# Moving part of w2's last block to an earlier load on 32 partitions, and w_mod in two loads

## The chip, the core and the metric

The kernel runs on one core of one Trainium2 chip. The metric is the time of one execution on the device in microseconds (us). Beside it each execution reports its *span*, the time from the first to the last recorded instruction of the core. Time minus span is called *overhead* below. The engines are named as in the profile: PE multiplies matrices, DVE and ACT work on vectors, POOL does small side work, SP issues the loads. A load is split over up to sixteen DMA engines; each moves its share in *packets* and, when it is through, posts a *landing* (in the trace of before, the load w2[16:24] has sixteen, from 411.48 to 413.60 us). The last landing of a load releases whoever waits for it (there PE starts at 413.65 us). All executions that were timed in rounds are counted as fast ones, and on one core there is no slower die to sort out.

## The reference, cut to what matters

```python
mod = (silu(c) @ w_mod).reshape(2, 6, 1, -1)            # w_mod: 1024 x 6144
h = layernorm(x) * (1 + ca) + sa                        # x: 2 x 1 x 1024
x = x + ga * attention(h, k_cache, v_cache, wq, wo)     # 32 heads on 4 KV heads, 32768 keys
h = layernorm(x) * (1 + cb) + sb
x = x + gb * (gelu(layernorm(h) @ w1 + b1) @ w2 + b2)   # w1: 1024 x 3584, w2: 3584 x 1024
```

Two rows of x go through one transformer block. Everything else is weights and cache: 178.3 MB have to be read, and each byte is used once.

## The kernel before

All large loads are issued by SyncE into one queue, in one fixed order, each as soon as its place in memory is free. w_mod comes first, in three loads of 1, 3 and 4 blocks of k. w2 comes last, in five.

```python
WMOD_ITEMS = ((0, 1), (1, 4), (4, 8))
W2_ITEMS = ((0, 8, 96), (8, 16, 112), (16, 24, 0), (24, 27, 16), (27, 28, 22))  # from block, to block, place
...
for k0, k1 in WMOD_ITEMS:
    add(("wmod", k0), [k1 - k0, 6 * DM], wm_v[:, k0:k1, :], k0 * 12 * KB)
# wq, then K and V of 8 groups, then wo, then w1
w2_v = B_w2.rearrange("(p j) n -> p j n", j=FT)          # FT = 28 blocks, DM = 1024
for m, (j0, j1, off) in enumerate(W2_ITEMS):
    add(("w2", m), [j1 - j0, DM], w2_v[:, j0:j1, :], off * KB)
```

The end of the kernel. Blocks 16 to 27 of w2 are used as weights of small matmuls with two columns; what follows is short and serial.

```python
for g in range(16, FT):
    m, j = w2_of[g]
    it = need("w2", m)                                    # waits for this load
    for k in range(KT8):                                  # KT8 = 8
        pe(lambda e, ...: e.matmul(psO[:, 2 * k:2 * k + 2], lhsT=w[:, j, k * 128:(k + 1) * 128], rhs=gT[:, g, 0:2],
                                   start=False, stop=(g == FT - 1), ...), ...)
dve(... mT = psO * mod(5));  dve(... res_bf = mT + x1b)
pe(... psM = res_bf transposed);  dve(... res16 = psM)
...
T.wait("sp", reads=["res16"])
T.raw("sp", lambda e: e.dma_start(out..., res16[:, :]).then_inc(s_out, 16))
...
nc.sync.wait_ge(s_out, 16)                                # the program ends when the output is in memory
```

Of the kernel before, what the change touches and what calls it, by code (L numbers as in the profile page):

```python
# [8 lines left out]
BF16 = mybir.dt.bfloat16  # L9
# [5 lines left out]
DM = 1024  # L15
KT8 = DM // 128
F = 3584
FT = F // 128
# [15 lines left out]
RING = 160 * 1024  # L34
KC_AT = 128 * 1024
AHEAD = ("sc2", "sc3", "pk", "ac")
WMOD_ITEMS = ((0, 1), (1, 4), (4, 8))
W2_ITEMS = ((0, 8, 96), (8, 16, 112), (16, 24, 0), (24, 27, 16), (27, 28, 22))
KEEP = {(0, 1): 0, (0, 3): 1, (0, 5): 2, (1, 1): 3}

# [196 lines left out]
def bass_adaLN_cond__gqa_block_cached__mixer_channel_mlp__decode_kernel(  # L237
# [15 lines left out]
    T = Tracker(nc)  # L253
    T.step["pe"], T.step["dve"] = 74, 18

    def sb(name, shape, dtype=FP32):
        return nc.alloc_sbuf_tensor(name, list(shape), dtype)

    ident = sb("ident", [128, 128], BF16)
# [41 lines left out]
    gT = sb("gT", [128, FT, 32], BF16)  # L301
    mT = sb("mT", [128, KT8, 2])
    res_bf = sb("res_bf", [128, 2, KT8], BF16)
    res16 = c16
    m1c = sb("m1c", [128, HPG, NCH])
    m1 = sb("m1", [128, HPG])
    gm = sb("gm", [HPG, 1])
# [25 lines left out]
    psO = psZ[:, 1, :]  # L333
    psM = nc.alloc_psum_tensor("psM", [128, 512], FP32)
# [8 lines left out]
    KB = 1024  # L343

    def add(key, shape, src, off, slot=None, sem=None, view=None):
        it = Item()
        it.key, it.n = key, len(stream)
        it.off, it.nbytes = off, int(np.prod(shape)) * 2
        assert off + it.nbytes <= RING
        it.reg = f"it{it.n}"  # L350
        it.sem = f"d_{sem or slot or it.reg}"
        it.view = views.get(slot) if view is None else view
        if it.view is None:
            it.view = nc.alloc_sbuf_tensor_at(f"{key[0]}_{it.n}", [128] + list(shape), BF16, offset=abase + off)
            if slot:
                views[slot] = it.view
        it.src = src
        stream.append(it)
        by_key[key] = it
# [31 lines left out]
        add(("w1", m), [4, F], w1_v[:, 4 * m:4 * m + 4, :], off * KB)  # L391
    w2_v = B_w2.rearrange("(p j) n -> p j n", j=FT)
    for m, (j0, j1, off) in enumerate(W2_ITEMS):
        add(("w2", m), [j1 - j0, DM], w2_v[:, j0:j1, :], off * KB)
    w2_of = {j: (m, j - j0) for m, (j0, j1, off) in enumerate(W2_ITEMS) for j in range(j0, j1)}

    kc = nc.alloc_sbuf_tensor_at("kc", [128, 2, TPC * D], BF16, offset=abase + KC_AT)
# [18 lines left out]
    def dve(fn, reads=(), writes=(), sem=None):  # L416
        T.inst("dve", fn, reads=reads, writes=writes, sem=sem)
# [4 lines left out]
    def pe(fn, reads=(), writes=(), mark=True):  # L422
        T.inst("pe", fn, reads=reads, writes=writes, mark=mark)
# [5 lines left out]
    for t, nm in ((ident, "ident"), (identf, "identf")):  # L429
        T.inst("pool", lambda e, t=t: e.memset(t[:, :], 0.0), writes=[nm])  # L430
        T.inst("pool", lambda e, t=t: e.affine_select(out=t[:, :], in_=t[:, :], compare_op=ALU.not_equal, fill=1.0,
                                                      base=0, pattern=[[-1, 128]], channel_multiplier=1), reads=[nm], writes=[nm])
    T.inst("pool", lambda e: e.memset(onesf[:, :], 1.0), writes=["onesf"])
    for t, nm in [(inT, "inT"), (gT, "gT")] + [(atT[g], f"atT{g}") for g in range(G // 2)]:
        T.inst("pool", lambda e, t=t: e.memset(t[:, :, :], 0.0), writes=[nm])

    for k in range(KT8):
        pe(lambda e, k=k: e.matmul(psM[:, 2 * k:2 * k + 2], lhsT=c2[:, k::KT8], rhs=ident[0:2, 0:2], start=True, stop=True),
           reads=["KT_sb0", "ident"], writes=["psM"], mark=False)
# [46 lines left out]
    for k in range(KT8):  # L486
        k0, kk = wmod_of[k]
        it = need("wmod", k0)
        for ch in range(12):
            n, q = ch // 4, ch % 4  # L490
            pe(lambda e, w=it.view, k=k, kk=kk, ch=ch, n=n, q=q: e.matmul(bank[n][32 * q:32 * q + 32, :], lhsT=inT[:, k, :], rhs=w[:, kk, ch * 512:(ch + 1) * 512],  # L491
                                                                   start=(k == 0), stop=(k == KT8 - 1), skip_group_check=True),
# [227 lines left out]
    for m in range(2):  # L720
        it = need("wo", m)
        for j in range(16):
            for hf in range(2):
# [2 lines left out]
                                                                       start=(m == 0 and j < 2), stop=(m == 1 and j >= 14), skip_group_check=True),  # L726
                   reads=[it.reg, f"atT{m}"], writes=["psS0"], mark=(j == 15 and hf == 1))

    def load_row(e_name, b, b_reg, n, parts=128):
        dst, src = row[0:parts, n * 512:(n + 1) * 512], b[0:parts, :]  # L730
        if e_name == "act":
            act(lambda e: e.activation(dst, src, ACT.Copy), reads=[b_reg], writes=[f"row{n}"] + ROW)
        else:
            dve(lambda e: e.tensor_copy(dst, src), reads=[b_reg], writes=[f"row{n}"] + ROW)

    def to_columns(dst, d_reg, n, start, mark):
        for i in range(4):
            pe(lambda e, i=i: e.matmul(dst[:, 2 * i:2 * i + 16].rearrange("p (h r) -> p h r", r=8)[:, :, 0:2], lhsT=row[:, n * 512 + i * 128:n * 512 + (i + 1) * 128],
                                       rhs=half[:, :, :], start=(start and i == 0), stop=True, skip_group_check=True),
               reads=[f"row{n}", "half"] + ROW, writes=[d_reg], mark=(mark and i == 3))  # L740
# [51 lines left out]
               reads=[it.reg, "gT"], writes=["psS0"], mark=(hf == 1 and g in (7, 15)))  # L792
    load_row("dve", psS[0], "psS0", 3)
    to_columns(psO, "psO", 3, True, False)
    for g in range(16, FT):
        m, j = w2_of[g]
        it = need("w2", m)
        for k in range(KT8):
            pe(lambda e, w=it.view, g=g, j=j, k=k: e.matmul(psO[:, 2 * k:2 * k + 2], lhsT=w[:, j, k * 128:(k + 1) * 128], rhs=gT[:, g, 0:2],  # L799
                                                            start=False, stop=(g == FT - 1), skip_group_check=True),  # L800
               reads=[it.reg, "gT"], writes=["psO"], mark=(k == KT8 - 1 and g in (23, 26, 27)))
    dve(lambda e: e.tensor_tensor(mT[:, :, :], psO[:, 0:16].rearrange("p (k b) -> p k b", b=2), mod(5), ALU.mult), reads=["psO", "modT"], writes=["mT"])
    dve(lambda e: e.tensor_tensor(res_bf.rearrange("p b k -> p k b"), mT[:, :, :], x1b[:, :, :], ALU.add), reads=["mT", "x1b"], writes=["res_bf"])
    pe(lambda e: e.matmul(psM[0:16, 0:128], lhsT=res_bf.rearrange("p b k -> p (b k)"), rhs=ident[:, :], start=True, stop=True),
# [38 lines left out]
```

## Time and profile before

| what | before |
|---|---|
| time, median of 3 (range) | 420.06 us (419.78 to 420.2) |
| span of the profiled execution | 419.0 us |
| bytes read | 178.28 MB, 425 GB/s over the span |
| latest landing of w2[16:24] | 413.60 us |
| from there to the end of the span | 5.40 us |
| instruction blocks fetched (16 KB each) | 8 |

The pages of the profile are read from the end backwards. The last row of work is a chain: the load w2[16:24] lands, PE works through 96 small matmuls, DVE multiplies and adds, PE transposes, DVE copies, and the 4 KB result is stored. Whatever moves the time must move the landing of w2[16:24], or something behind it. The lines themselves stand in the prediction below.

### The profile page before, as it was taken

What the parts mean: (1) busy time and instruction counts of PE and PEld (TensorE: products, weight loads), DVE (VectorE), ACT (ScalarE), POOL (GpSimd) and SP (SyncE); (2) the same over time, 40 slices, a digit from 0 to 9 for tenths busy, and PEclk for the clock granted to TensorE, in tenths of its full rate; (3) what the DMA queues carried; (4) which work ended last, traced back from release to release, by engine and by line L of the source; (5) the groups of instructions that cost most, each with busy time, mean ns of one, the idle gap of its engine ahead of it and who ended that gap; (6) DMA issues with size and microseconds to landing.
All of it is one profiled execution on the core that took longest, in us unless ns stands there. A gap on an engine that the chain in (4) does not pass through costs nothing.

```text
span 419.0 us, 11898 instructions
## 1 busy us (share of the span) xinstructions
PE 291.7 (70%) x5215; PEld 234.7 (56%) x5215; DVE 246.1 (59%) x535; ACT 181.8 (43%) x219; POOL 6.8 (2%) x29
## 2 busy tenths in 40 slices
PE   1407445878599578939885995798398839966466
PEld 1104114874499378719854993687198539932324
DVE  1201101856786877778577768777885868683421
ACT  2000012555277537715862775378248716750100
POOL 3000000000000000000000000000000000000000
PEclk9966656798799969988987999699889968996565
DMA  9999999999999999999999999999999999999995
GB/s 369 448 391 443 444 408 491 408 409 460 413 432 450 419 432 450 438 413 450 438 413 457 432 413 457 432 413 463 432 407 463 432 407 463 404 416 443 422 429 230
DMA packets 4573, 178.42 MB, mean 426 GB/s; under 512 B 586, under 2 KB 594, under 8 KB 852
## 3 DMA queue, kind: packets, MB, share of 16 engines
q1 hardware_dynamic: 4564, 178.28, 98.6%
q8 instruction: 8, 0.13, 0.1%
q14 instruction: 1, 0.01, 0.0%
HBM read 178.28 MB, written 0.00 MB: 425 GB/s over the span
## 4 chain that ended last, share of the span: by engine, by line
DMA 60%; PE 22%; DVE 9%; issue 5%; ACT 3%; SPq 0%; ACTq 0%; DVEq 0%
DMA kv<-in_A_k_cache_dram 45%; PE psKT L560 13%; DMA wmod<-in_w_mod_dram 7%; DMA w<-in_B_w_dram 7%; ACT KT_sb L564 3%; DVE KT_sb L566 3%; PE psS L577 2%; DVE m1c L581 2%; DVE kc L571 2%; PE psZ L629 1%; PE psZ L577 1%; DVE msum L652 1%; PE psS L725 1%; PE psZ L491 1%; PE psZ L799 1%
## 5 line engine op out<-in xcount | busy, mean ns | idle before, releaser
L564 ACT ACTIVATE KT_sb<-psKT 128x1024 bf16<-128x1024 bf16 x128 | 128.3, 1024 | 96.7 <-PE psKT L560 96.7
L566 DVE COPY KT_sb<-psKT 128x1024 bf16<-128x1024 bf16 x128 | 88.0, 689 | 59.7 <-PE psKT L560 59.4
L560 PE MATMUL psKT<-ident,kv 128*128 128x128 bf16 x1024 | 90.5, 248 | 10.9 <-DMA kv<-in_A_k_cache_dram 10.9
L560 PEld LDWEIGHTS psKT<-ident,kv 128*128 128x128 bf16 x1024 | 73.3, 113 | 12.8 <-DMA kv<-in_A_k_cache_dram 12.8
L560 PE MATMUL psKT<-ident,kc 128*128 128x128 bf16 x1024 | 77.9, 218 | 0.0
L560 PEld LDWEIGHTS psKT<-ident,kc 128*128 128x128 bf16 x1024 | 58.1, 97 | 1.9 <-issue 1.7
L577 PE MATMUL psS<-qcur,KT_sb 128*128 128x8 bf16 x1024 | 45.1, 167 | 10.1 <-DVE KT_sb L566 6.0
L577 PE MATMUL psZ<-qcur,KT_sb 128*128 128x8 bf16 x1024 | 42.1, 167 | 11.2 <-ACT KT_sb L564 10.7
L577 PEld LDWEIGHTS psS<-qcur,KT_sb 128*128 128x128 bf16 x1024 | 40.2, 98 | 11.9 <-DVE KT_sb L566 6.3
L577 PEld LDWEIGHTS psZ<-qcur,KT_sb 128*128 128x128 bf16 x1024 | 36.8, 96 | 13.4 <-ACT KT_sb L564 12.7
L571 DVE COPY kc<-kv 128x4096 bf16<-128x4096 bf16 x32 | 39.0, 1217 | 8.1 <-DMA kv<-in_A_k_cache_dram 8.1
L629 PE MATMUL psZ<-V,E_sb 128*32 128x512 bf16 x384 | 28.3, 414 | 2.0 <-ACT E_sb L603 2.0
L603 ACT ACTIVATE E_sb<-S_sb 128x512 bf16<-128x512 f32 x32 | 19.2, 626 | 16.1 <-DVE S_sb L601 16.1
L601 DVE TENSOR_TENSOR S_sb<-S_sb,gmb 128x512 f32<-128x512 f32 x32 | 21.3, 687 | 0.5
L642 PE MATMUL psM<-onesf,rsum 128*128 128x1 f32 x16 | 3.4, 281 | 25.9 <-DVE rsum L639 25.9
L608 DVE TENSOR_REDUCE rs<-E_sb 128x8 f32<-128x512 bf16 x32 | 20.9, 675 | 0.0
L642 PEld LDWEIGHTS psM<-onesf,rsum 128*128 128x128 f32 x16 | 2.7, 212 | 29.9 <-DVE rsum L639 29.9
L582 ACT ACTIVATE S_sb<-psS 128x512 f32<-128x512 f32 x16 | 9.6, 597 | 20.4 <-DVE m1c L581 20.4
L491 PE MATMUL psS<-wmod,inT 128*32 128x512 bf16 x32 | 4.9, 606 | 17.0 <-DMA wmod<-in_w_mod_dram 17.0
L629 PEld LDWEIGHTS psZ<-V,E_sb 128*32 128x32 bf16 x384 | 11.0, 102 | 9.5 <-ACT E_sb L603 2.7
L657 PE MATMUL psM<-msum,hmat 128*128 128x128 f32 x16 | 6.4, 501 | 13.3 <-DVE msum L652 13.3
L499 DVE COPY S_sb<-psS 128x512 f32<-128x512 f32 x1 | 0.7, 692 | 23.2 <-PE psS L491 23.2
(139 smaller groups left out, 237.4 us busy)
## 6 DMA issues: line engine op xcount, KB each, us to landing
wq<-in_A_wq_dram SPq DMA_DIRECT2D x2, 4096.0 KB, 44.7
kv<-in_A_k_cache_dram SPq DMA_DIRECT2D x2, 4096.0 KB, 37.7
wo<-in_A_wo_dram SPq DMA_DIRECT2D x2, 4096.0 KB, 20.6
w<-in_B_w_dram SPq DMA_DIRECT2D x2, 3584.0 KB, 23.5
wmod<-in_w_mod_dram SPq DMA_DIRECT2D x1, 6144.0 KB, 29.9
w<-in_B_w_dram SPq DMA_DIRECT2D x3, 2048.0 KB, 29.2
wmod<-in_w_mod_dram SPq DMA_DIRECT2D x1, 4608.0 KB, 15.9
wmod<-in_w_mod_dram SPq DMA_DIRECT2D x1, 1536.0 KB, 6.2
```

Of the source, the lines that this page charges most:

```text
L491: pe(lambda e, w=it.view, k=k, kk=kk, ch=ch, n=n, q=q: e.matmul(bank[n][32 * q:32 * q + 32, :], lhsT=inT[:, k, :], rhs=w[:, kk, ch * 512:( ...
L560: pe(lambda e, kq=kq, jj=jj, w=kt, t=t: e.transpose(psKT[kq][:, jj * 128:(jj + 1) * 128], w[:, t, :], ident[:, :]), reads=[k_reg, "ident"] ...
L564: act(lambda e, src=src: e.activation(KT_sb[g8][:, :, :], src, ACT.Copy), reads=[f"psKT{kq}"], writes=[f"KT_sb{g8}"], sem=f"ev{cc}_{g8}")
L566: dve(lambda e, src=src: e.tensor_copy(KT_sb[g8][:, :, :], src), reads=[f"psKT{kq}"], writes=[f"KT_sb{g8}"], sem=f"ev{cc}_{g8}")
L571: dve(lambda e: e.tensor_copy(kc[:, n // 2, lo:lo + 32 * D], kv[:, 2 + n // 2, lo:lo + 32 * D]), reads=[it.reg], writes=[f"kc{n}"], sem=f" ...
L577: pe(lambda e, t=t, jj=jj: e.matmul(ps[:, t * HPG:(t + 1) * HPG], lhsT=KT_sb[g8][:, jj, :], rhs=qcur[:, :], start=True, stop=True), reads= ...
L581: dve(lambda e: e.tensor_reduce(m1c[:, :, cc], ps.rearrange("p (t h) -> p h t", h=HPG), AX.X, ALU.max), reads=[preg], writes=[f"m1c{cc}"], ...
L582: act(lambda e: e.activation(Sc, ps.rearrange("p (t h) -> p h t", h=HPG), ACT.Copy), reads=[preg], writes=[f"S_sb_{cc}"], sem=f"sc{cc}")
L601: dve(lambda e: e.tensor_tensor(Sc, Sc, gmb[:, part, :].unsqueeze(2).to_broadcast([128, HPG, TPC]), ALU.subtract), reads=[f"S_sb_{cc}", f" ...
L603: act(lambda e: e.activation(Ec, Sc.rearrange("p h (u t) -> p u h t", t=4), ACT.Exp, scale=SCALE), reads=[f"S_sb_{cc}"], writes=[f"E_sb_{c ...
L608: dve(lambda e: e.tensor_reduce(dst, Ec.rearrange("p u h t -> p h u t"), AX.XY, ALU.add), reads=[f"E_sb_{cc}"], writes=[reg])
L629: pe(lambda e, t4=t4, tg=tg, q=q: e.matmul(acc[32 * q:32 * q + 32, :], lhsT=E_sb[:, tg // 4, :, :].rearrange("p h t -> p (h t)"), rhs=vt[: ...
```

## The change

The title of the change also names a two-part softmax and 64 KB packets for K; the kernel before has both. What the diff does:

- The last block of w2 is cut. Its first 640 columns stay in the last load. The other 384 columns (3/8) are loaded earlier, ahead of w1, into a tile `w2x` that lies on partitions 0 to 31 only, by four loads of 32 rows each. Each of these has an outer size of 4: four DMA engines in place of sixteen. A load has 24 KB, the four together 98 KB. The intent is apparently to give bytes to engines that reach the end of the stream early, and to lighten the load that all wait for at the end.
- Because `w2x` has 32 partitions, the columns of gT that belong to those rows have to be gathered onto 32 partitions: four small matmuls with a selection matrix and one copy.
- w_mod comes in two loads instead of three.

```diff
-WMOD_ITEMS = ((0, 1), (1, 4), (4, 8))
+WMOD_ITEMS = ((0, 3), (3, 8))
+W2_CUT = 640
...
+        n1 = W2_CUT if j1 == FT else DM
+        add(("w2", m), [j1 - j0, n1], w2_v[:, j0:j1, 0:n1], off * KB)
...
+    for q in range(4):
+        src = w2_v[32 * q:32 * q + 32, FT - 1, W2_CUT:DM].rearrange("(b a) n -> a b n", a=4)
+        T.dma("sp", lambda e, ...: e.dma_start(w2x[:, q, :], src), key=f"ld_w2x{q}", writes=[f"w2x{q}"])
...
+    for q in range(4):
+        pe(... e.matmul(psM[0:32, 56 + 2 * q:58 + 2 * q], lhsT=selp[:, 32 * q:32 * q + 32], rhs=gT[:, FT - 1, 0:2], ...), ...)
+    dve(... gx = psM[0:32, 56:64])
     for g in range(16, FT):
...
+        if g == 24:
+            for q in range(4):
+                for k in range(W2_CUT // 128, KT8):
+                    pe(... e.matmul(psO[:, 2 * k:2 * k + 2], lhsT=w2x[:, q, ...], rhs=gx[:, q, :], ...), ...)
-        for k in range(KT8):
+        for k in range(KT8 if g < FT - 1 else W2_CUT // 128):
```

Cut from it: the tiles' allocation, the selection matrix built on GpSimd at the start, and the flags of the accumulation.

More of the change, by code (lines that the diff above doesn't have):

```diff
@@ L304, in bass_adaLN_cond__gqa_block_cached__mixer_channel_mlp__decode_kernel @@
     res16 = c16
+    w2x = sb("w2x", [32, 4, DM - W2_CUT], BF16)
+    gx = sb("gx", [32, 4, 2], BF16)
+    selp = sb("selp", [128, 128], BF16)
     m1c = sb("m1c", [128, HPG, NCH])
@@ L393, in bass_adaLN_cond__gqa_block_cached__mixer_channel_mlp__decode_kernel @@
     for m, (j0, j1, off) in enumerate(W2_ITEMS):
-        add(("w2", m), [j1 - j0, DM], w2_v[:, j0:j1, :], off * KB)
+        n1 = W2_CUT if j1 == FT else DM
+        add(("w2", m), [j1 - j0, n1], w2_v[:, j0:j1, 0:n1], off * KB)
     w2_of = {j: (m, j - j0) for m, (j0, j1, off) in enumerate(W2_ITEMS) for j in range(j0, j1)}
@@ L433, in bass_adaLN_cond__gqa_block_cached__mixer_channel_mlp__decode_kernel @@
     T.inst("pool", lambda e: e.memset(onesf[:, :], 1.0), writes=["onesf"])
+    T.inst("pool", lambda e: e.tensor_copy(selp.rearrange("p (q a b) -> p q a b", q=4, a=4), ident.rearrange("p (q b a) -> p q a b", q=4, a=4)),
+           reads=["ident"], writes=["selp"])
     for t, nm in [(inT, "inT"), (gT, "gT")] + [(atT[g], f"atT{g}") for g in range(G // 2)]:
@@ L727, in bass_adaLN_cond__gqa_block_cached__mixer_channel_mlp__decode_kernel @@
                    reads=[it.reg, f"atT{m}"], writes=["psS0"], mark=(j == 15 and hf == 1))
+    for q in range(4):
+        src = w2_v[32 * q:32 * q + 32, FT - 1, W2_CUT:DM].rearrange("(b a) n -> a b n", a=4)
+        T.dma("sp", lambda e, q=q, src=src: e.dma_start(w2x[:, q, :], src), key=f"ld_w2x{q}", writes=[f"w2x{q}"])
     def load_row(e_name, b, b_reg, n, parts=128):
@@ L794, in bass_adaLN_cond__gqa_block_cached__mixer_channel_mlp__decode_kernel @@
     to_columns(psO, "psO", 3, True, False)
+    for q in range(4):
+        pe(lambda e, q=q: e.matmul(psM[0:32, 56 + 2 * q:58 + 2 * q], lhsT=selp[:, 32 * q:32 * q + 32], rhs=gT[:, FT - 1, 0:2],
+                                   start=True, stop=True), reads=["selp", "gT"], writes=["psM"], mark=(q == 3))
+    dve(lambda e: e.tensor_copy(gx[:, :, :], psM[0:32, 56:64].rearrange("p (q b) -> p q b", b=2)), reads=["psM"], writes=["gx"])
     for g in range(16, FT):
@@ L797, in bass_adaLN_cond__gqa_block_cached__mixer_channel_mlp__decode_kernel @@
         it = need("w2", m)
-        for k in range(KT8):
+        if g == 24:
+            for q in range(4):
+                for k in range(W2_CUT // 128, KT8):
+                    pe(lambda e, q=q, k=k: e.matmul(psO[:, 2 * k:2 * k + 2], lhsT=w2x[:, q, k * 128 - W2_CUT:(k + 1) * 128 - W2_CUT], rhs=gx[:, q, :],
+                                                    start=False, stop=False, skip_group_check=True),
+                       reads=[f"w2x{q}", "gx"], writes=["psO"], mark=False)
+        for k in range(KT8 if g < FT - 1 else W2_CUT // 128):
             pe(lambda e, w=it.view, g=g, j=j, k=k: e.matmul(psO[:, 2 * k:2 * k + 2], lhsT=w[:, j, k * 128:(k + 1) * 128], rhs=gT[:, g, 0:2],
-                                                            start=False, stop=(g == FT - 1), skip_group_check=True),
-               reads=[it.reg, "gT"], writes=["psO"], mark=(k == KT8 - 1 and g in (23, 26, 27)))
+                                                            start=False, stop=(g == FT - 1 or (g == FT - 2 and k >= W2_CUT // 128)), skip_group_check=True),
+               reads=[it.reg, "gT"], writes=["psO"], mark=((k == KT8 - 1 and g in (23, 26)) or (g == FT - 1 and k == W2_CUT // 128 - 1)))
     dve(lambda e: e.tensor_tensor(mT[:, :, :], psO[:, 0:16].rearrange("p (k b) -> p k b", b=2), mod(5), ALU.mult), reads=["psO", "modT"], writes=["mT"])
```

## The prediction

> **What bounds the kernel now.** I read the page first (engine shares, the 40 slices), then the table by stretch, then the chain of waits in order of time, and last the trace's own records of DMA packets and landings for the first 8 us and the last 5.
>
> The shares of the whole span, then busy time of each engine by stretch (columns: stretch, length, PE, weight loads, DVE, ACT, POOL, granted clock, DMA share, GB/s):
>
> ```profile
> PE 291.7 (70%) x5215; PEld 234.7 (56%) x5215; DVE 246.1 (59%) x535; ACT 181.8 (43%) x219; POOL 6.8 (2%) x29
> ...
> 0.00:8.00 8.00, 0.66 (x9) 0.59 (x9) 0.18 (x1) 1.69 (x3) 3.27 (x13) 1.00 0.89 345
> 8.00:38.00 30.00, 11.35 (x100) 4.19 (x100) 4.45 (x17) 1.69 (x3) 0.00 (x0) 0.77 1.00 431
> ...
> 112.00:370.00 258.00, 204.32 (x4054) 179.31 (x4056) 192.44 (x386) 149.36 (x177) 3.09 (x14) 0.90 1.00 433
> 370.00:411.00 41.00, 25.12 (x261) 11.08 (x253) 16.76 (x63) 5.21 (x10) 0.25 (x1) 0.69 1.00 430
> 411.00:413.60 2.60, 1.87 (x8) 1.78 (x8) 0.43 (x1) 0.00 (x0) 0.00 (x0) 0.50 0.94 393
> 413.60:416.50 2.90, 2.82 (x96) 2.71 (x96) 0.00 (x0) 0.00 (x0) 0.00 (x0) 0.50 0.31 122
> ```
>
> From 8 us to 411 us the sixteen DMA engines are busy all the time (share 1.00, some 433 GB/s) and no compute engine reaches 80%. So 178.3 MB of loads set the time; compute in the middle is free. Only three things can move it: the bytes and packets on the slowest DMA engine, the start before the stream is full, and the tail after the last large landing. The whole change lies in the start and the tail. (Two-part softmax and 64 KB K packets, named in the change's title, are in the kernel before already: it has two maxima, and the trace holds 1,920 packets of 65,536 bytes. The diff does not touch them.)
>
> The tail, from the chain of waits in order of time (columns: start, length, what):
>
> ```profile
> 384.35 29.25 DMA w<-in_B_w_dram
> 413.60 0.05 issue
> 413.65 2.83 PE psZ L799 x96
> 416.48 0.02 issue
> 416.50 0.19 DVE mT L802
> ```
>
> The chain leaves the DMA at 413.60 and runs on PE for all 96 matmuls; it does not return to the DMA for the last block of w2. The landing records say why. Each load posts one landing per DMA engine. Load w2[16:24] has its sixteen between 411.48 and 413.60 us, w2[24:27] between 413.37 and 415.41, w2[27] between 414.02 and 416.02. PE starts matmuls 26.7 ns apart: 64 from 413.646 to 415.35, waits some 0.08 us longer than its cadence for 415.41, does 24 more, and comes to the last block at 416.115, when that has been there for 0.1 us. So the last load, which the change makes lighter, ends no wait now; the load ahead of it costs 0.08 us.
>
> [...] the bias loads with 1, 2, 4 and 1 rows show 1, 2, 4 and 1 data landings, all by 361.32 us, while the V load just before them lands on its late group of six engines from 361.71 on. [...] Here eight such packets of 0.88 to 0.96 us lie in the span (at 36, 62, 83, 90, 97, 104, 387 and 409 us), and each is followed by a hole of 0.87 to 0.95 us in an engine's packets. That is most of the 2.0 us between first and last landing. [...]
>
> **The change part by part.**
>
> *Last block of w2.* The main load goes from 2,048 to 1,280 bytes a row, eight rows an engine. Packets on one engine follow each other every 80 ns at 2,048 bytes and 37 ns at 896; between them (an estimate) 51 ns at 1,280 and 32 ns at 768. Every engine saves 8 x (80 - 51) = 0.23 us on its last load, so the latest landing goes from 416.02 to about 415.79. [...] So three landings of w2 keep their times, and only the fourth, which ends no wait, is 0.23 us earlier.
>
> *PE in the tail.* Removed: 3 matmuls of the last block. Added: 12 on the 32-partition pieces and 4 that pick rows of gT. The 4 fit between the fp32 matmuls that end at 413.35 and the landing at 413.60, with their copy beside PE. The 12 stand between g = 23 and g = 24. From 413.646 PE has 64 + 12 + 24 + 5 = 105 matmuls: 104 x 26.7 ns = 2.77, and 0.19 for the last to end, is 2.96 us. Before it was 2.82 with the 0.08 us wait, which the 12 now fill. So the tail costs **+0.14 us**: the landing wait is bought off with more matmul time than it was worth. The added waits are on loads long landed; the already satisfied wait for the second half of wo added nothing to the cadence of 107 ns a matmul, so I count none.
>
> *w_mod in two loads.* An engine moves 8 packets of 36,864 and 8 of 61,440 bytes in place of 8 each of 12,288, 36,864 and 49,152. A packet costs about 7 ns beside its bytes (460 ns for 12,288, 1,815 for 49,152), so 8 fewer save 0.06 us, and one semaphore record less some 0.01. The 12,288-byte packets average 541 ns in place of 460, all of it in the first one or two of each engine (667 to 1,439 ns where 460 is normal): 8 x 81 = 0.65 us an engine. I take that for the cost of starting, which stays with large packets too; perhaps a seventh of it goes. Sum **-0.15 us**, through the whole stream.
>
> What else moves there is hidden. x and c queue behind 36 KB packets and land near 13 us, not 6.9, so PE starts w_mod near 14.5 and ends its first three k by 19. The second load brings five k in place of four at 32.3 us: 12 more matmuls of 107 ns, 1.28 us. PE then had 4.7 us to spare before wq's second half (52.69), and the first K load lands at 62.3 with qT there since 58.0. The loads behind it are issued 15 to 30 us before their turn, so 1.3 us later starves nothing.
>
> *Copies on POOL, 3 KB more SBUF.* At the start and beside other work: nothing.
>
> Sum: 420.06 + 0.14 - 0.15 = about **420.0 us**.
>
> **Rivals.** (1) The last landing ends the kernel, and the cut gives its full 0.23 us: 419.7. Against it: the chain never returns to the DMA after 413.60. [...] (3) The slow first packets go away with large ones: up to 0.5 us more, 419.5. For it: 1,364 ns exactly for each 36,864-byte packet later; against it, they come later, when the stream is running. (4) 26 more PE instructions cross a block border and bring a ninth fetch ahead of the last loads: +0.9 us. Little speaks for it: only some 240 are left after the fetch at 409.
>
> **Range and chances.** Every path moves less than 1 us of 420, and the three runs of before spread 0.42 us. I say 420.0 us, 419.4 to 420.7 in 8 of 10. Two per cent is 8.4 us, which no rival comes near: 0.01 faster, 0.98 within, 0.01 slower.
>
> **What would show it.** In the changed profile the last PE group of the chain should be unbroken, some 2.9 to 3.0 us from the landing of w2[16:24] to the DVE multiply, with 105 matmuls. The last load's latest landing should come over 0.4 us before PE asks for it. The four small loads should take near 1.0 us on four engines and leave the latest landing of w2[16:24] where the stream puts it, within 0.2 us of 413.5. w_mod should be complete by 32.2 us, and slices 2 to 38 should look alike. Wrong would be: a DMA entry in the chain after w2[16:24], a landing of w2[16:24] past 414 with w_mod on time, or w_mod complete by under 31.9.

No term of the sum is cut: it came to 420.06 + 0.14 - 0.15 = about 420.0 us. Two steps are needed below; by what the trace shows they are these. The first is the cost of the four small loads. Loads of 1, 2 and 4 rows posted 1, 2 and 4 data landings in the trace of before, so four engines were expected to take the new loads of outer size 4, with 32 packets of 768 bytes each: at the estimated 32 ns, 1.03 us on each of the four, ahead of w1. Of the sixteen landings of w2[16:24] eight came by 412.15 us and eight from 412.62 on; from some 412.2 the four would come to 413.2, before 413.60. That the four are among the early ones was the assumption, drawn from the early landings of the bias loads, and the step to "three landings of w2 keep their times" rests on it. The second is rival 2: one of the four also takes one of the two late instruction blocks (387 and 409 us), its w2[16:24] lands near 414.2, PE starts 0.6 us late, and the time is 420.6. The "eight such packets" are those of the instruction queue, 16,384 bytes each. The "semaphore record" was costed like the 4-byte packets of the load queue, 546 in the trace of before with a median of 9 ns.

## The result, and the profile after

| | before | after |
|---|---|---|
| time, median of 6 (range) | 420.13 us (419.78 to 420.52) | 422.13 us (420.87 to 423.27) |
| ratio, 95% interval | | 1.0047, 1.0028 to 1.0065 |
| span of the profiled execution | 419.0 us | 419.6 us |

The kernel became slower by half a per cent. In the terms of 2% it is "the same", as predicted; the 422.13 us lie outside the predicted range of 419.4 to 420.7. Ratios here are always the mean time of one kernel's fast runs over that of the other's fast runs of the same rounds, so they are not quite the ratio of the medians quoted beside them.

Two things stand out before any line is read. The profiled execution of the changed kernel is its fastest one, 420.87 us, so the profile shows less than the loss. And the six executions spread over 2.4 us, where the kernel before spread over 0.74.

The shares, the instruction queue, and the table by stretch of the changed kernel (columns: stretch, length, PE, weight loads, DVE, ACT, POOL, granted clock, DMA share, GB/s):

```profile
PE 289.0 (69%) x5228; PEld 233.7 (56%) x5228; DVE 246.3 (59%) x536; ACT 181.9 (43%) x219; POOL 7.0 (2%) x30
...
q8 instruction: 9, 0.15, 0.1%
...
0.00:8.00 8.00, 0.00 (x0) 0.00 (x0) 0.00 (x0) 1.28 (x1) 3.49 (x14) 1.00 0.84 327
8.00:38.00 30.00, 10.72 (x109) 4.76 (x109) 4.67 (x18) 1.91 (x4) 0.00 (x0) 0.83 1.01 435
...
112.00:370.00 258.00, 204.10 (x4066) 178.82 (x4067) 192.67 (x386) 149.96 (x178) 3.09 (x14) 0.90 1.00 433
370.00:411.00 41.00, 23.73 (x249) 10.17 (x240) 15.82 (x61) 4.68 (x9) 0.26 (x1) 0.71 1.00 422
...
413.60:416.50 2.90, 2.85 (x96) 2.74 (x96) 0.15 (x1) 0.00 (x0) 0.00 (x0) 0.50 0.46 184
416.50:419.60 3.10, 0.81 (x21) 0.54 (x18) 0.68 (x3) 0.00 (x0) 0.00 (x0) 0.50 0.03 7
```

Four readings. The first 38 us moved 8 x 327 + 30 x 435 = 15.67 MB in place of 8 x 345 + 30 x 431 = 15.69 MB: w_mod in two loads brought nothing forward. The middle is unchanged at 433 GB/s. Between 370 and 411 us the DMA share is still 1.00, but 422 GB/s came out of it where it was 430: the engines were as busy, and moved less. Last, the instruction queue fetched nine blocks in place of eight.

The end of the chain in order of time (columns: start, length, what):

```profile
383.88 29.96 DMA w<-in_B_w_dram
413.84 0.05 issue
413.89 1.87 PE psZ L820 x64
415.76 0.41 PE psZ L816 x12
416.17 0.88 PE psZ L820 x29
417.05 0.02 issue
417.07 0.19 DVE mT L823
```

The landing of w2[16:24] ended the wait 0.24 us later than in the profile of before. PE then took from 413.890 to 417.070, which is 3.18 us; before it took from 413.646 to 416.504, which is 2.86 us.

### The profile page after: what moved, and what is told of

It is laid out like the page before. It is cut to its first block, busy times and chain, and to the rows that moved or that the text cites. A ratio compares the mean times of both kernels' runs of the same rounds, so it can differ in the third digit from the quotient of the medians.

```text
span 419.6 us, 11930 instructions
## 1 busy us (share of the span) xinstructions
PE 289.0 (69%) x5228; PEld 233.7 (56%) x5228; DVE 246.3 (59%) x536; ACT 181.9 (43%) x219; POOL 7.0 (2%) x30
## 4 chain that ended last, share of the span: by engine, by line
DMA 54%; PE 25%; DVE 11%; issue 6%; ACT 4%; SPq 0%; ACTq 0%; DVEq 0%
DMA kv<-in_A_k_cache_dram 39%; PE psKT L567 14%; DMA wmod<-in_w_mod_dram 7%; DMA w<-in_B_w_dram 7%; ACT KT_sb L571 3%; DVE KT_sb L573 2%; PE psS L584 2%; DVE m1c L588 2%; DVE kc L578 2%; PE psZ L636 2%; DVE msum L659 2%; PE psZ L584 2%; DVE rs L615 1%; PE psS L732 1%; PE psZ L498 1%
## 5 line engine op out<-in xcount | busy, mean ns | idle before, releaser
L664 PE MATMUL psM<-msum,hmat 128*128 128x128 f32 x16 | 6.4, 502 | 13.3 <-DVE msum L659 13.3
L589 ACT ACTIVATE S_sb<-psZ 128x512 f32<-128x512 f32 x16 | 9.6, 599 | 9.2 <-DVE m1c L588 8.1
L588 DVE TENSOR_REDUCE m1c<-psZ 128x8 f32<-128x512 f32 x16 | 11.0, 689 | 3.4 <-PE psZ L584 3.4
```

Of the source, the lines that this page charges most:

```text
L588: dve(lambda e: e.tensor_reduce(m1c[:, :, cc], ps.rearrange("p (t h) -> p h t", h=HPG), AX.X, ALU.max), reads=[preg], writes=[f"m1c{cc}"], ...
L589: act(lambda e: e.activation(Sc, ps.rearrange("p (t h) -> p h t", h=HPG), ACT.Copy), reads=[preg], writes=[f"S_sb_{cc}"], sem=f"sc{cc}")
```

## The experiments

Every kernel ran on one chip beside the kernel before, most with five rounds. "Slow packets" and landings below are from the trace's own DMA records: a packet counts as slow if it took over 13% longer than the usual time of its size, and "excess" is the sum of what was too long over all engines. The kernel before has none of these where w1 begins. (One packet of w1 near 387 us is slow in every kernel, with 1,556 ns in the kernel before; it runs beside an instruction block and is left out.) The changed kernel has 20 to 24 of them, all between 379.5 and 383.5 us, 16 or 17 at the same time, so on all sixteen engines: packets of 28,672 bytes of w1, which normally take 1,062 ns, took up to 1,542 ns in the first profile. In that stretch `w2x` is being loaded. This is the suspect of the first experiments.

### The change again, and its two halves

e0 is the change unchanged. e1 is the kernel before with w_mod in two loads only; e2 is the change with w_mod in three loads.

```diff
 # e1, against before
-WMOD_ITEMS = ((0, 1), (1, 4), (4, 8))
+WMOD_ITEMS = ((0, 3), (3, 8))
 # e2, against the change
-WMOD_ITEMS = ((0, 3), (3, 8))
+WMOD_ITEMS = ((0, 1), (1, 4), (4, 8))
```

> The changed kernel as it is, for a second profile: the first fell on its fastest run (420.87 us of 420.87 to 423.27). Theory A (the four small loads of w2, on four DMA engines, slow the loads that run beside them on all engines): packets beside the small loads near 380 us take up to 1.5 us where 1.06 is normal, and the last landing of w2[16:24] is over 414.5 us in a run of 422 us. Theory B (w_mod in two loads disturbs the start): the first K load lands over 1 us later than the 62.3 us of before. Both: 422 us.

> The kernel before with only w_mod in two loads. Theory A: 419.8 to 420.4 us, like before, and a spread under 0.8 us. Theory B: 421.5 us or more, spread over 2 us.

> The changed kernel with w_mod in three loads as before: only the w2 part. Theory A: 421.5 to 423 us and a spread over 2 us. Theory B: 420.1 to 420.6 us (the longer PE tail alone).

| run | median (range), us | before | ratio, 95% |
|---|---|---|---|
| e0 | 421.22 (421.05 to 422.75) | 419.89 | 1.0039, 1.0023 to 1.0055 |
| e1 | 419.94 (419.83 to 420.54) | 419.89 | 0.9998, 0.9985 to 1.0011 |
| e2 | 421.99 (421.03 to 422.46) | 419.89 | 1.0047, 1.0034 to 1.0061 |

The loss repeats, and all of it belongs to w2. w_mod in two loads is worth nothing: its last landing came at 32.39 us against 32.30 before, and the slow first packets cost 0.70 us an engine where they cost 0.65.

### Sixteen engines into the same 32 partitions

e3 loads the rows in their natural order. The source then has an outer size of 32, sixteen engines share it (sixteen landings for each load in the trace), and the destination is still partitions 0 to 31.

```diff
-        src = w2_v[32 * q:32 * q + 32, FT - 1, W2_CUT:DM].rearrange("(b a) n -> a b n", a=4)
+        src = w2_v[32 * q:32 * q + 32, FT - 1, W2_CUT:DM]
...
-        pe(... lhsT=selp[:, 32 * q:32 * q + 32] ...)
+        pe(... lhsT=ident[:, 32 * q:32 * q + 32] ...)
```

> The changed kernel, but the four small loads take their rows in natural order, so that each is split over sixteen DMA engines (2 packets of 768 bytes each) and not over four (8 each). If it is the crowding on four engines that slows the others: 420.2 to 420.8 us, no packets over 1.2 us near 380 us. If it is small strided reads as such, wherever they run: 421.5 us or more.

Measured: 421.18 us (420.87 to 422.28), ratio 1.003 (1.0017 to 1.0043), with 23 slow packets and 8.3 us of excess. It makes no difference to the slow packets whether four engines load these rows or sixteen. So the four engines as such are not their cause. (The expectation had either no slow packets or 421.5 us and more; neither came.)

### One load on all partitions

e6 loads the same 384 columns, at the same place in the queue, as one load of 128 partitions, and uses them in 3 matmuls of full height. Its result is right.

```diff
-    w2x = sb("w2x", [32, 4, DM - W2_CUT], BF16)
+    w2x = sb("w2x", [128, DM - W2_CUT], BF16)
...
-    for q in range(4): ... T.dma(... dma_start(w2x[:, q, :], src) ...)
+    T.dma("sp", lambda e: e.dma_start(w2x[:, :], w2_v[:, FT - 1, W2_CUT:DM]), key="ld_w2x", writes=["w2x"])
...
-            for q in range(4): for k in range(5, 8): matmul(lhsT=w2x[:, q, ...], rhs=gx[:, q, :])
+            for k in range(5, 8): matmul(lhsT=w2x[:, ...], rhs=gT[:, FT - 1, 0:2])
```

> The same 384 columns at the same place in the queue, but as one load to all 128 partitions[...]; as many matmuls as before, right result. If packets near 380 us are slowed because 4 or 16 engines crowd on partitions 0 to 31: no packet over 1.2 us there apart from an instruction packet, 419.7 to 420.0 us. If the short strided reads slow the memory: packets of 1.3 to 1.5 us again, 420.2 to 420.5.

Measured: 420.38 us (419.95 to 421.78) against 419.8, ratio 1.0013 (0.9995 to 1.0032). No packet was slow, and w2[16:24] landed at 413.29. Equal bytes in equally small rows of 768 bytes, read equally far apart, make no packet slow when they go to all partitions. Its time is not told apart from that of before, though the median lies 0.6 us higher and outside the expected 419.7 to 420.0. It does not beat the kernel before: lightening the last load won nothing that shows.

### The loads without their matmuls

Two kernels were refused by a check for races before they reached a chip: e5, the loads alone, and e7, the same with the reads from contiguous memory. Nothing waited for the four loads by the end of the program. They were mended as e8 and e9, in which SyncE waits for the loads just ahead of the output's store, when they have been there for 30 us. Both give a wrong result, since the 384 columns are loaded and not used.

```diff
 # e8, against the change
-    for q in range(4): pe(... selp ...)
-    dve(... gx ...)
...
-        if g == 24: (the 12 matmuls on w2x)
...
-    T.wait("sp", reads=["res16"])
+    T.wait("sp", reads=["res16"] + [f"w2x{q}" for q in range(4)])
 # e9, against e8
-        src = w2_v[32 * q:32 * q + 32, FT - 1, W2_CUT:DM].rearrange("(b a) n -> a b n", a=4)
+        src = B_w2[12 * q:12 * q + 12, :].rearrange("r n -> (r n)").rearrange("(b a n) -> a b n", a=4, b=8)
```

> The changed kernel without its 16 added PE matmuls and their copy (result wrong on purpose): the loads alone, 3 matmuls fewer than before. Theory A: the whole loss, 420.8 us or more, spread over 1.5. Theory F: eight instruction packets, spread under 1.2, and only the slowing of packets near 380 us, some 0.4 us less 0.1 on PE: 420.0 to 420.4.

> The loads alone, to partitions 0 to 31 on four engines as in the change, but read from one contiguous piece of w2 each (result wrong on purpose). If the crowded partitions slow the stream: packets of 1.3 to 1.5 us near 380 us as in the loads alone, same time. If the reads 57 KB apart do: no slow packets, 0.3 to 0.5 us less than the loads alone.

> The changed kernel without its 16 added PE matmuls and their copy (result wrong on purpose); the end waits for the four loads, long landed. Crowding theory (four engines write into partitions 0 to 31[...], and all loads beside them slow down): packets of 1.3 to 1.5 us near 380 us, landing of w2[16:24] 0.4 to 0.7 us later than before, span 419.0 to 419.3 against some 418.6 in most runs of before, time 420.3 to 420.7. Rival (the loss is on PE): 419.8.

> As the loads alone, but each of the four loads reads one contiguous piece of w2 (result wrong on purpose). Crowding theory: the same slow packets near 380 us and the same time as the loads alone. Rival (reads 57 KB apart slow the memory; weakened by the run that read the same columns to 128 partitions without one slow packet): no slow packets, 0.3 to 0.5 us less.

e8: 420.56 us (420.46 to 421.76), ratio 1.002 (1.0007 to 1.0034), 21 slow packets, 7.6 us of excess, w2[16:24] at 414.05. e9: 420.58 us (420.5 to 422.48), ratio 1.002 (1.0006 to 1.0034), 20 slow packets, 7.45 us. So the loads cost some 0.7 us by themselves: four of e8's five spans lie at 419.2 to 419.4, where the kernel before has 418.6. (Its PE tail, with three matmuls fewer, is 2.79 us where before has 2.86.) How far apart the rows lie in memory has nothing to do with it. Two of e9's executions and one of e8's were slower by over 0.9 us for another reason: in e9's profile one engine was 1.1 us behind the second latest from 387 us on, after being late already on the last V load. What held it was not found.

### Four engines into partitions 0 to 15 and 32 to 47

e10 changes where the rows go. It makes eight loads of 16 rows, into partitions 0 to 15 and 32 to 47, in place of four of 32 rows into partitions 0 to 31. The rows in between are zero, and the matmuls have full height. The author chose these partitions by an assumption about which engine writes which rows of a load of 128 partitions, and called them the engines' own; the records of packets hold no partition and no engine number, so no run shows that. The result is right, and the bytes and the packets are those of the change, 32 small ones on each of four engines. Partitions written are 32 here too; what differs is which, and that each load is cut in two, and no run separates those.

```diff
-    w2x = sb("w2x", [32, 4, DM - W2_CUT], BF16)
+    w2x = sb("w2x", [128, 4, DM - W2_CUT], BF16)          # set to zero once, at the start
...
     for q in range(4):
-        src = w2_v[32 * q:32 * q + 32, ...].rearrange("(b a) n -> a b n", a=4)
-        T.dma(... dma_start(w2x[:, q, :], src) ...)
+        for h in range(2):
+            src = w2_v[32 * q + 16 * h:32 * q + 16 * h + 16, ...].rearrange("(b a) n -> a b n", a=4)
+            T.dma(... dma_start(w2x[32 * h:32 * h + 16, q, :], src) ...)
```

> The same columns and bytes on the same four engines[...] (eight loads of 16 rows; the other rows are zero, and the matmuls use all 128 rows). Right result. Crowding theory: no slow packets near 380 us, landing of w2[16:24] back near 413.3, four engines about 1.0 us later. Rival (four short-packet engines slow the rest wherever they write): slow packets stay. For PE: if the 0.07 us gaps before and after the 12 matmuls come from their 32-row form, they go: 2.98 us from the landing to the multiply; if from their waits, 3.18 as in the change. Time 420.1 to 420.5, or 421 and more for the rival.

Measured: 420.67 us (420.35 to 421.05), ratio 1.0016 (1.0002 to 1.0029), spans 419.0 to 419.4. Not one packet was slow, though the time is not back at that of before; the 32 small packets of an engine took 36 ns each, 1.15 us an engine where the prediction had 1.03. (In the change they took 1.36 us an engine.) The next lines show the stretch in which `w2x` is loaded, 379 to 383 us (columns as above; the last is GB/s), first of the kernel before:

```profile
379.00:383.00 4.00, 3.02 (x26) 1.42 (x30) 1.57 (x5) 0.00 (x0) 0.25 (x1) 0.50 0.97 417
```

of the change:

```profile
379.00:383.00 4.00, 3.49 (x30) 1.58 (x34) 1.14 (x4) 0.00 (x0) 0.26 (x1) 0.50 0.96 347
```

of e8, the loads without their matmuls:

```profile
379.00:383.00 4.00, 2.63 (x22) 1.26 (x26) 1.93 (x6) 0.00 (x0) 0.25 (x1) 0.50 0.98 355
```

and of e10:

```profile
379.00:383.00 4.00, 3.53 (x30) 1.58 (x34) 1.10 (x4) 0.00 (x0) 0.25 (x1) 0.50 0.92 390
```

The DMA share stays near 1 in all of them, so this is not idle time. In the two kernels that write partitions 0 to 31 the rate falls by 60 to 70 GB/s for four microseconds; in e10 by 27, with a lower share. A window of 4 us cuts large packets at its ends, so the count of slow packets (about 21, 21 and 0) is the cleaner figure.

e10 answers a second question. The chain's end of e10:

```profile
383.85 29.70 DMA w<-in_B_w_dram
413.55 0.05 issue
413.59 1.87 PE psZ L824 x64
415.46 0.32 PE psZ L820 x12
415.78 0.79 PE psZ L824 x29
416.57 0.02 issue
416.59 0.18 DVE mT L827
```

The same 105 matmuls take 3.00 us in e10 and 3.18 us in the change. The tile view of the 12 added matmuls says what differs; the change first:

```profile
L816 PE MATMUL psZ<-gx,w2x x12: 160/160/182, 415.7 to 416.0; 32*128 32x2 bf16 x12
```

then e10:

```profile
L820 PE MATMUL psZ<-gx,w2x x12: 165/165/165, 415.3 to 415.6; 128*128 128x2 bf16 x12
```

In the change they use 32 rows of the array between matmuls that use 128. The steps of the chain show it: 0.41 us for twelve against 0.32 us, and 0.88 against 0.79 for the 29 after them. In the records the pause at the first of them is 97 + 49 ns and at the first one after them 93 + 47 ns, where two steps of the usual 26.7 ns would be 53: near 0.09 us each. In e10 the step is 26 to 27 ns from the one group to the other and back.

### The added matmuls alone, and moved forward

e4 is the kernel before with 13 tiny matmuls at 403 to 405 us, where PE waits anyway. It asks whether more PE instructions, which bring a ninth instruction block, cost anything.

```diff
+    for n in range(13):
+        pe(lambda e: e.matmul(psM[0:32, 56:58], lhsT=ident[:, 0:32], rhs=ident[:, 0:2], start=True, stop=True), ...)
     for g in range(16):
```

> The kernel before with 13 tiny matmuls more on PE (as many as the change adds), put where PE waits for gT at 403 to 405 us; no load is touched. Theory F (26 more PE instructions bring a ninth 16 KB block of instructions, which comes late and holds PE or the end up in some runs): nine instruction packets, some runs 0.7 to 1.5 us longer, median 420.3 to 421.5. Theory A (the small loads alone slow the stream): 419.9 us as before, spread under 1.2.

e4: 420.1 us (419.74 to 420.17), ratio 0.9998 (0.9981 to 1.0014). The ninth block came, at 416.49 us, and cost nothing. At this point I took the block to be harmless; e15 to e17 below took that back for a block that comes later.

e11 is the change with the 4 selecting and 12 added matmuls ahead of the wait for w2[16:24]; e12 does the same to e10.

```diff
+    (the 4 matmuls with selp and the copy to gx, here)
     for g in range(16): ...
     to_columns(psO, "psO", 3, True, False)
+    (the 12 matmuls on w2x, here)
     for g in range(16, FT):
-        if g == 24: (the 12 matmuls on w2x)
```

> The changed kernel with its 4 + 12 matmuls moved ahead of the wait for w2[16:24], where PE idles. Sizes the PE part of the loss: 2.75 to 2.8 us from that landing to the multiply against 3.18 in the change and 2.86 before, so 0.35 to 0.4 us less than the change: 420.7 to 421.0, the slow packets near 380 us as in the change. If PE is no part of the loss: 421.1 to 421.3 as the change.

> [...] the 4 + 12 matmuls ahead of the wait for w2[16:24]: the change with both found losses taken out. No slow packet near 380 us; about 2.78 us from the landing of w2[16:24] to the multiply (2.86 before, 3.00 with the own rows alone); span 418.7 to 419.0 in most runs, 419.9 to 420.3 us. No run with a span over 420.2, if such runs come from the crowding; one or two in five, if they come from four engines being late.

e11: 421.72 us (420.43 to 422.19), ratio 1.0042 (1.0028 to 1.0056). PE took 2.73 us after the landing in place of 3.18, and the median did not improve (420.7 to 421.0 was expected): four of its five executions were late by the count given below. None of the four was profiled, so the cause in them is not shown; the fifth, which was, shows eight instruction blocks. e12: 420.5 us (419.99 to 420.54) against 420.02, ratio 1.0008 (0.9994 to 1.0021), with PE at 2.79 us and no slow packet. e12 ties with the kernel before. It is the best form of the idea that was found, and it wins nothing.

### The loads twice

e13 issued each of the four loads a second time into a second tile. It did not build: there was no memory left for the tile (the last one to be placed needed 2,048 bytes, and 1,792 were left). e14 is the same with the unused selection matrix taken out. Its result is wrong, as e8's.

```diff
+    w2y = sb("w2y", [32, 4, DM - W2_CUT], BF16)
...
         T.dma("sp", ... e.dma_start(w2x[:, q, :], src), key=f"ld_w2x{q}", ...)
+        T.dma("sp", ... e.dma_start(w2y[:, q, :], src), key=f"ld_w2y{q}", ...)
```

> The loads alone, each issued twice into two places of partitions 0 to 31 (result wrong on purpose): the suspected cost doubled. Crowding theory: 40 to 46 slow packets near 380 us in place of 20 to 23 and 15 us of packet time too much, summed over the engines, in place of 7.6; landing of w2[16:24] 0.5 to 1.2 us later than with the loads once; 421.1 to 422 us. If the slow packets have another cause near 380 us: some 20 as before, and 420.6 us plus what the bytes cost, under 0.3.

> The loads alone, each issued twice into two places of partitions 0 to 31 (result wrong on purpose; the unused selection tile is left out for room): the suspected cost doubled. Crowding theory: 40 to 46 slow packets near 380 us in place of 20 to 23 and 15 us of packet time too much, summed over the engines, in place of 7.6; landing of w2[16:24] 0.5 to 1.2 us later than with the loads once; 421.1 to 422 us. If the slow packets have another cause near 380 us: some 20 as before, and 420.6 us plus what the bytes cost, under 0.3.

Measured: 422.31 us (422.15 to 422.94) against 419.9, ratio 1.0056 (1.0042 to 1.007); 32 slow packets, 13.3 us of excess where e8 had 7.6; w2[16:24] at 415.60. Twice the loads into these partitions make 1.75 times the excess. That is less than the expected 40 packets and 15 us, and the time is above the expected 421.1 to 422 us. The time grows by more than twice (spans 420.7 to 421.5, e8 419.3, before 418.6), but here the four engines also carry another 32 small packets each, so this run doubles two things at once and does not size them one by one.

### Why some executions are slower still

Undisturbed executions of the change have a span of 419.6 to 420.1 us and an overhead of 1.3 us. Many have one or the other, or both, larger, by up to 2.4 us. Four looks at the change, e15a to e15d, were to catch such an execution in a profile.

> The changed kernel, one look. In a fast execution: span 419.5 to 420.0 us, 20 to 23 slow packets, 7.2 to 8.4 us of packet time too much. In a slow one (span over 420.6): crowding that lasts longer gives 12 us or more of it; an instruction packet on an engine already late gives 7 to 8.5 us as ever, and one engine whose landing of the first half of w1 or of w2[16:24] is 0.8 us or more behind the second latest.

> The changed kernel, a second look; expectations as for the first.

> The changed kernel, a third look; expectations as for the first.

> The changed kernel, a fourth look; expectations as for the first.

They took 422.83, 421.05, 421.13 and 421.97 us, with spans of 421.5, 419.8, 419.8 and 419.5. e15a is a late one, e15b an undisturbed one. Neither of the two explanations in the expectation was it: e15a has 20 slow packets and 7.4 us of excess, and no engine is far behind the others at w1 or w2[16:24]. The chain's PE steps of e15a:

```profile
414.23 1.87 PE psZ L820 x64
...
416.51 0.88 PE psZ L820 x29
```

and the same steps of e15b:

```profile
414.07 1.87 PE psZ L820 x64
...
416.35 0.88 PE psZ L820 x29
```

Up to here the two are 0.16 us apart. The rest of the 1.7 us lies behind. SyncE's waits at the end (columns: total, times, longest, in us) and the issue of the output's store (its size, and the time from issue to landing), in e15a:

```profile
SPq L835 <- DMA out_dram<-c: 2.2, 1, 2.2
...
out_dram<-c SPq DMA_DIRECT2D x1, 4.0 KB, 3.0
```

and in e15b:

```profile
SPq L835 <- DMA out_dram<-c: 0.6, 1, 0.6
...
out_dram<-c SPq DMA_DIRECT2D x1, 4.0 KB, 1.4
```

The store of 4 KB took 3.0 us in place of 1.4. Fifteen of its sixteen landings in e15a were there by 419.88 us; one came at 421.50. What else was moving: the ninth instruction block, one packet of 16 KB that started at 419.17 us and took 1,295 ns. Fifteen of the store's sixteen packets of 256 bytes started between 419.37 and 419.51 us, the last at 420.45, just as the instruction packet ended. In e15d this packet started at 420.83, after the span's end, took 1,375 ns, and the overhead was 2.47 us. The change added 13 instructions to PE and 13 weight loads (5,228 of each where there were 5,215), which put the border of a block there: nine were fetched where there were eight. In the eight profiles of the change, e2 and e3 the ninth block started at 417.2 to 418.0 us in five, none of them late, and at 419.2 to 420.8 us in three: e15a and e15d, both late, and e0 (420.44 us), which was not. Why it comes at two places was not found.

If that is so, moving the border must take the late executions away, in either direction. e16 is the change with 20 PE matmuls fewer elsewhere (a wrong result: the bias of w1 and the last k of w_mod are left out). e17 is the change with 20 more, idle ones, at 403 to 405 us; its result is right.

```diff
 # e16, against the change
+        if k == KT8 - 1: continue          # w_mod's last k: 12 matmuls
...
-    for q in range(4): for n in range(2): pe(... b1m ...)   # 8 matmuls
 # e17, against the change
+    for n in range(20):
+        pe(lambda e: e.matmul(psM[0:32, 56:58], lhsT=ident[:, 0:32], rhs=ident[:, 0:2], start=True, stop=True), ...)
     for g in range(16):
```

> The changed kernel without 20 PE matmuls elsewhere (the 8 that add b1, the 12 of w_mod's last k; result wrong on purpose), so fewer PE instructions than before the change; loads as in the change. Theory of the ninth block: eight instruction packets, no execution with a time over 1.45 us above its span, none or one of six with a span over 420.4; median 420.9 to 421.2, spread under 0.8. If the loads make the slow executions: two of six with a span over 420.6 as in the change, spread over 1.2.

> The changed kernel with 20 tiny PE matmuls more, at 403 to 405 us where PE waits. Right result. Theory of the ninth block: its packet comes at 416.2 to 417.2 us and is through before the store at 418.3, so although instructions were added no execution is over 1.45 us above its span or over 420.4 us in span; median 420.9 to 421.2. If the loads make the slow executions: as the change, 421.2 to 422.1 median, spread over 1.2.

| run | median (range), us | before | ratio, 95% | late executions | ninth block |
|---|---|---|---|---|---|
| change, first result | 422.13 (420.87 to 423.27) | 420.13 | 1.0047, 1.0028 to 1.0065 | 5 of 6 | 417.2 to 420.8 us (six profiles) |
| e16, 20 fewer | 421.01 (420.93 to 421.26) | 420.1 | 1.0021, 1.0008 to 1.0035 | 0 of 5 | none |
| e17, 20 more | 420.86 (420.84 to 421.58) | 420.1 | 1.0018, 1.0005 to 1.0032 | 0 of 5 | 417.07 us |

An execution is counted as late here if its span is 1.2 us or more above its kernel's lowest (419.5 for all runs of the change), or its overhead is above 1.45 us. Over the first result, e0, e2, e3, e11 and the four looks 20 of 32 executions are late; of e16 and e17 none of 10, although e17 has more work than the change. In e17's profile the ninth block ends at 418.03 us and the store is issued at 418.88. That the place of the border makes most of the late executions is thus shown by moving it. That the block stands in front of the store's share on one DMA engine is what the last packet and the one late landing in e15a suggest; which engine fetched it the records don't number. Late executions with a large overhead are seen in two profiles, e15d and e10, both with the block behind the span's end; e0 has the same and is not late, so how the block lengthens the overhead is not shown.

The count does not explain everything. Beside those kernels, e10, whose ninth block came at 420.13 us, has 2 of 5 late (overheads of 1.87 and 2.05), as the account would have it. But e12, with its block at 416.76 us, has 2 of 5 with an overhead of 1.6, and without any ninth block e14 has 2 of 6 (overheads of 1.46 and 1.50) and e6, e8 and e9 one each, by their span.

The kernel before has late executions too, 5 of 61 by the same count, 3 of them with a span of 419.8 us or more. It has no ninth block, and why it has them stays open.

## Why the prediction was wrong

It was wrong in time (420.0 predicted, 422.13 measured), right in class. By its own steps:

**What bounds the kernel: right.** The DMA stream is the bound up to 411 us, the middle did not move, and the chain is unbroken PE work after w2[16:24]. The time from that landing to the end of the span, read from each profile with spans rounded to 0.1 us, is a yardstick for the rest:

| kernel | w2[16:24] landed | span | difference |
|---|---|---|---|
| before | 413.60 | 419.0 | 5.40 |
| e6, all partitions | 413.29 | 418.7 | 5.41 |
| e10, partitions 0 to 15 and 32 to 47 | 413.55 | 419.1 | 5.55 |
| e12, as e10, early | 413.85 | 419.2 | 5.35 |
| e8, loads only | 414.05 | 419.4 | 5.35 |
| the change | 413.84 | 419.6 | 5.76 |
| the change, e15a | 414.19 | 421.5 | 7.31 |

**"So three landings of w2 keep their times": this step failed.** The four small loads were costed by the 1.03 us that they take on the four engines. What they do to the other twelve was not asked. Written into partitions 0 to 31 they slow all sixteen engines at once for four microseconds (packets of up to 1,542 ns in place of 1,062), 7.2 to 8.3 us of packet time in sum, near 0.5 us an engine, and no engine is spared, so the stream as a whole comes later: the earliest landing of w1's first half went from 388.42 to 388.87. The latest of w2[16:24] came at 413.84 us in the fastest execution and at 414.23 in e0's profile, past the 413.5 ± 0.2 that the prediction gave and, in e0, past the 414 that it named as a sign of being wrong. The slow packets come with how the loads lie on the partitions (20 to 24 of them on 0 to 31, none in e6 and e10), not with the number of engines (e3), the reads (e9), the bytes (e6, e10) or PE (e8). That it matters which engine writes which partition was the assumption and is not shown; e10 also cuts each load in two. Why writing into partitions 0 to 31 slows all sixteen engines is not shown either. In time, the loads cost 0.7 us (e8). e10 has spans 0.5 us above those of before, of which its PE tail is 0.15; e12 has 0.2. So the slow packets are, as an estimate from these spans, about 0.4 us of the 0.7. The remaining 0.2 to 0.4 us, which e10 and e12 still have, may be the four engines' extra packets, 1.15 us an engine in e10 (so rival 2, given below the prediction, stays open), or the added bytes ahead of w1; no run separates those.

**"So the tail costs +0.14 us": right as a mechanism, too small as a term.** The count was right: 105 matmuls, at the predicted cadence, and e10, where these are of full height, takes 3.00 us, with 0.15 us more behind the landing than before. The change takes 3.18 us. The term left out is the switch from 128 rows to 32 and back, near 0.09 us each way. The term for the tail is thus +0.32 us, not +0.14. The trace shows the two pauses (97 + 49 and 93 + 47 ns, where two steps are 53) and not what PE does in them.

**Rival 4 was the one that came true, for another reason than the one given.** It had a ninth fetch "ahead of the last loads: +0.9" and was dismissed because few instructions are left after the eighth. The fetch came behind the last loads, at 417 to 421 us, where it meets the store of the result. In e16 and e17, which in their profiles have no fetch while the store is under way, the ratio is 1.0021 and 1.0018, some 0.8 to 0.9 us; with it the change has 1.0039 to 1.0047, some 1.6 to 2.0 us. So it makes about 0.7 to 1.2 us of the mean (an estimate from these ratios), and between nothing and 2.4 us of a single execution.

**"Sum -0.15 us" for w_mod: this step failed too.** e1 measured 0.9998 with an interval of 0.26% in all, and its last landing was not earlier but 0.09 us later. The gain rested on a seventh of the start cost going away, and that cost stayed whole (0.70 us an engine against 0.65). One small reading was off too: 460 and 1,815 ns give some 8 ns beside a packet's bytes, not 7, which changes nothing here.

**The hidden parts: right.** The 1.28 us of later w_mod matmuls starved nothing, the last load landed at 416.09 before PE asked for it, and the cut of its 0.23 us had no effect, as the chain had said; rival 1 was rightly set aside.

The sum of undisturbed executions: 418.6 + 0.7 (loads, e8) + 0.4 (PE, 3.18 us against e8's 2.79) = 419.7, and 419.6 to 420.1 is what they show. To this come up to 2.4 us in somewhat over half of the executions, most of which the ninth block's place explains.

## What to carry to other kernels

The cost of a small load on a busy stream is not only its own packets: loads of 98 KB into partitions 0 to 31 slowed packets on all sixteen engines here (up to 1,542 ns in place of 1,062), and the same bytes on all 128 partitions, or in halves on 0 to 15 and 32 to 47, slowed none; so compare the durations of the neighbours' packets, and try other partitions. A handful of added instructions (13 matmuls and their weight loads) moved the border of an instruction block into the last microseconds here, where its fetch met the output's store (3.0 us in place of 1.4); look at the number and the place of the instruction packets, and try the kernel with some idle matmuls more or fewer when the times of one kernel spread. When the chain already says that the last load ends no wait, expect nothing from making that load lighter: here its 0.23 us brought nothing.
